# Weight folds turned by TensorE instead of through DRAM, and a new order of all stages, in a kernel of two linear-attention layers and two expert layers

## The chip, the cores and the metric

The kernel runs on one core of a Trainium2 chip. The metric is the device time of one execution in microseconds (us), the median of several runs. The engines are TensorE (PE in the profile, its weight loads PEld), VectorE (DVE), ScalarE (ACT), GpSimd (POOL) and SyncE (SP), which here only issues transfers (DMAs).

## The reference

A batch of one, 2048 rows x of width 576, passes four layers, A, B, A, B, with the same weights in both A and in both B. All arithmetic is fp32.

```python
def A(x):                                  # linear attention, 32 heads of 18
    q, k, v = heads(layernorm(x) @ wqkv)
    pq, pk = phi(q), phi(k)                # phi(t) = (t + 1 if t > 0 else exp(t)) + 1e-6
    kv = einsum("bhsd,bhse->bhde", pk, v)  # a sum over all 2048 rows
    z = pk.sum(over rows)
    o = einsum("bhqd,bhde->bhqe", pq, kv) / (einsum("bhqd,bhd->bhq", pq, z) + 1e-6)
    return x + rows(o) @ wo

def B(x):                                  # 32 heads choose one of 8 x 8 experts each
    y = layernorm(x)
    q = einsum("nd,dhc->nhc", y, w_q)      # two halves of 128 per head
    s1, s2 = q[..., :128] @ k1.T, q[..., 128:] @ k2.T
    e = 8 * argmax(s1) + argmax(s2)        # per row and head; the softmax over one choice is 1
    out = einsum("nhk,nhk,nhkd->nd", 1, gelu(y . u[e]), v[e])
    return x + out
```

## The kernel before

The 2048 rows are cut into 16 tiles of 128 rows (t = 0 to 15). Layers A and B of a pair are joined into "layer" l = 0 or 1 in the names, so that a name such as `x10_9` is buffer x1 of layer 0, tile 9. In a layer A first all tiles give their share of the state (stages f, k, v, st, and q, whose result pq waits in DRAM or in the core); when the state is complete, it is multiplied into the output weight (M), and the tiles go on one by one: ld (loads of x and pq), num (division by the denominator), oT (o is turned), O (output product and residual, x1), bT (layernorm, turned), S (scores of layer B), sel and gel (choice of expert, gelu), cT (the 64 coefficients turned), po (product with the expert values, residual x2), keep (x2 stored to DRAM). As soon as a tile of layer 0 is through, its layer-1 front (f, k, v, st) can follow.

Precision: a product of fp32 operands is done as products of halves. `split` makes them: hi is a rounded copy on ACT (L117), lo the difference on DVE (L118). A projection of a tile is 14 passes of two column parts, 28 matmuls: `ppk`, `ppv`, `ppq` (L258), `ppo` of O (L483). S is 14 matmuls (L525, its PSUM tile is called `kva` or `pps` in the profile), the state `kva` is L360, po L609.

TensorE needs the rows turned (columns on the partitions). There are two ways, and a table by tile chooses between them. `transposed`: five transposes on TensorE (L215) into PSUM, then the split. `squares`, by way of `moved`: DVE transposes the 32 x 32 squares (L229, result `r...`), one store (L231) of 320 KB takes them to DRAM (`y_d...`), four loads (L237) of 80 KB bring them back in another place (`g...`), then the split. So `rb`, `y_db`, `gb`, `thib`, `tlob` are the steps of operand b, `ro` ... `tloo` of o, `rf` ... `tlof` of f. In layer 0 the operand b goes by squares for tiles 5, 7, 9, 11 and 13.

The weights of S are made by the kernel itself: w_q (loaded in 64 pieces by `fold_load`, L631) is multiplied with the keys (`fold_mm`, L641, `fold_ps` in PSUM), in four chunks. `fold_out` (piece `fo`) copies a chunk to the core's memory (`foldf`, ACT L647 to L649), turns it by `moved` (`rfold`, `y_dfold`, `gfold`), and splits it to `shi` (ACT, L658) and `slo` (DVE, L662 and L664).

The order is written out by hand. `in_order(*ALL)` holds PE, ACT, DVE and POOL to the order of the program, and SP issues transfers in the order of the program too, one after the other. `play(text)` takes a list of pieces, "name layer.tile", and runs the next step (up to the next yield) of each, or n steps for "xn". There are four parts: a Python loop for the front tiles 2 to 9, then three texts: front tiles 10 to 15 and back tiles 0 to 4; a text that is played four times, for s = 5, 7, 9, 11 (numbers are relative to s, two tiles a turn); and the rest, with all of the second layer.

PSUM has four tiles of 128 x 1024; one holds the state while it is summed up, the others rotate.

Of the kernel before, what the change touches and what calls it, by code (L numbers as in the profile page):

```python
# [64 lines left out]
def network(ctx, tc, x_in, wqkv, wo, wq_t, k_t, u_t, v2, c_mask, c_mask4, c_ident, c_code, c_code1, c_scale, c_shift, out):  # L65
    nc = tc.nc
# [781 lines left out]
    with in_order(*ALL):

        play("""  # L850
            fT0.11 v0.10 k0.10 fT0.11x2 v0.10 fl0.13 fo0.3 ln0.13 ln0.12 fo0.3 q0.10 v0.10 q0.10 fT0.12 k0.11 k0.10
            v0.11 fT0.12 fT0.13 v0.11x2 q0.11 k0.11 fo0.3 fT0.12 st0.11 fT0.13 st0.10 fl0.15 lv0.0 fl0.14 k0.12 q0.11
            ln0.15 ld0.1 k0.12 fT0.13 v0.12x2 ln0.14 q0.12 fT0.14 q0.13 fT0.15 k0.13 fT0.14 v0.12 q0.12 k0.13 v0.13
            fT0.14 q0.13 k0.14 v0.13 fT0.15 v0.14 v0.13 st0.13 fT0.15 k0.14 st0.12 k0.15 sv0.0 ld0.0 v0.15 wl0.0 v0.14
            k0.15 v0.14 st0.14 v0.15x2 st0.15 mk0.0 zs0.0x2 num0.1 num0.0 M0.2x2 M0.3 ld0.2 num0.1 M0.3 num0.0x2 M0.1
            q0.14 oT0.0 num0.1 M0.1 num0.2 ld0.3 M0.0 M0.4 oT0.0 M0.0 oT0.1 M0.4 num0.2 oT0.1 O0.0x4 ld0.4 num0.2 O0.1
            oT0.2 num0.3 O0.1 num0.4 bT0.0 oT0.2 num0.3 bT0.0 O0.2 O0.1 S0.0 num0.3 num0.4 q0.14 O0.1 oT0.3 O0.2 ld0.6
            S0.0 bT0.1 ld0.5 num0.4 O0.2 gel0.0 sel0.0 oT0.3 sel0.0 bT0.1 q0.15 O0.2 sel0.0 gel0.0 q0.15 S0.1 O0.3
            sel0.0 S0.1 sel0.1x2 cT0.0 bT0.2 cT0.0 O0.3 num0.5 ld0.7 oT0.4 po0.0x2 gel0.1 bT0.2 S0.2 gel0.1 po0.0
            oT0.4 S0.2 sel0.1x2 O0.4 O0.3 sel0.2 po0.0 gel0.2 cT0.1 fT1.0 cT0.1 sel0.2 fT1.0 po0.1 gel0.2 v1.0 po0.1  # L860
            O0.3 sel0.2 po0.1 sel0.2 cT0.2 bT0.3 O0.4 bT0.3 po0.1 O0.4 k1.0 v1.0 cT0.2 k1.0 fT1.1 num0.5 fT1.1 S0.3
            po0.2 keep1.0 S0.3 po0.2 sel0.3x2 k1.1 num0.6 gel0.3 po0.2 v1.0 sel0.3 gel0.3 k1.1 v1.1 O0.4 bT0.4 sel0.3
            cT0.3 po0.2 v1.1x2 fT1.2 num0.6 num0.5 cT0.3 bT0.4 oT0.5 S0.4 oT0.5 O0.5 num0.6 fT1.2 st1.0 S0.4 O0.5x2
            keep1.1 st1.1 oT0.6 po0.3 oT0.6 keep1.2 O0.5
        """)
# [9 lines left out]
    with in_order(*ALL):

        play("""
            po0.11 gel0.12 bT0.13 sel0.12 po0.11x2 num0.15 sel0.12 v1.10 sel0.12 fT1.11 bT0.13 gel0.12 sel0.12 oT0.14
            k1.10 fT1.11 k1.10 v1.10 cT0.12 v1.10 num0.15 O0.14 num0.15 oT0.15 cT0.12 bT0.13 fT1.11 po0.12 S0.13
            po0.12x2 S0.13 oT0.15 O0.14 sel0.13x2 v1.11 gel0.13 O0.14 po0.12 fT1.12 gel0.13 oT0.15 O0.14 sel0.13x2  # L880
            k1.11 v1.11 O0.15 fT1.12 bT0.14 O0.15 cT0.13 st1.10 v1.11 cT0.13 bT0.14 S0.14 fT1.12 k1.11 po0.13 O0.15
            S0.14 gel0.14 po0.13 gel0.14 po0.13 keep1.12 k1.12 v1.12 sel0.14 st1.11 sel0.14 ldx1.3 po0.13 fT1.13
            sel0.14 k1.12 O0.15 v1.12 sel0.14 v1.12 cT0.14 bT0.15 cT0.14 bT0.15 po0.14 st1.12 po0.14 S0.15 fT1.13
            po0.14 fT1.13 S0.15 v1.13 ldx1.1 sel0.15 po0.14 fT1.14 v1.13 sel0.15x2 gel0.15 k1.13 gel0.15 sel0.15
            fT1.14 cT0.15 bT0.-1 v1.13 cT0.15 v1.14 po0.15 bT0.-1 k1.13 q1.13 v1.14 po0.15 q1.13 po0.15x2 ldq1.13
            v1.14 k1.14 wl1.0 st1.13 fT1.15x2 k1.15 v1.15 k1.14 rl1.0 st1.14 k1.15 v1.15x2 st1.15 rl1.1 lq1.0 mk1.0
            lq1.0 zs1.0 M1.1x2 zs1.0 rl1.3 M1.4x2 M1.3 num1.13 lq1.1 M1.0 ldx1.0 num1.0 num1.13 num1.0x2 M1.3 keep1.11
            lq1.1 num1.1 oT1.0 M1.0 oT1.0 num1.1 M1.2x2 rl1.2 rl1.4 lq1.2 O1.0 num1.1 oT1.1 num1.13 oT1.13 q1.14 lq1.2
            O1.0 oT1.1 O1.0x2 lq1.3 num1.2 q1.14 lq1.3 oT1.13 bc1.0,-9 O1.1 bc1.0,-9 num1.2 num1.3 O1.1 num1.2 S1.0
            oT1.2 S1.0 num1.3 oT1.2 lq1.4 ldx1.5 gel1.0 num1.3 O1.1x2 O1.2 bc1.1,-9 sel1.0 gel1.0 ldx1.2 sel1.0 lq1.4  # L890
            O1.13 bc1.1,-9 num1.4 rl1.6 sel1.0 num1.4 S1.1 ldx1.13 lq1.6 O1.2x2 num1.4 rl1.5 O1.13 rl1.7 S1.1 sel1.0
            O1.2 sel1.1 O1.13 ldq1.14 gel1.1 bc1.2,0 lq1.5 rl1.8 oT1.4 bc1.2,0 lq1.6 oT1.3 sel1.1x2 O1.13 gel1.1 S1.2
            oT1.3 po1.0 lq1.5 sel1.1 po1.0 S1.2 O1.3 sel1.2 rl1.9 num1.6 O1.3 bc1.13,1 num1.5 lq1.7 gel1.2 bc1.13,1
            sel1.2 num1.5 gel1.2 num1.5 oT1.4 S1.13 lq1.7 O1.3x2 rl1.11 sel1.2 po1.1 sel1.2 oT1.5 q1.15 ldx1.4 po1.1
            bc1.3,2 num1.6 S1.13 gel1.13 oT1.5 num1.6 ldx1.6 bc1.3,2 rl1.10 ldx1.7 sel1.13 q1.15 O1.4 po1.2 num1.14
            O1.5 po1.2 oT1.6 sel1.13 O1.4x2 ldq1.15 sel1.13 num1.7 S1.3 num1.14 num1.7 gel1.13 num1.14 S1.3 sel1.13
            O1.4 O1.5 sel1.3 lq1.8 num1.7 ldx1.14 sel1.3 oT1.6 gel1.3 bc1.4,13x2 O1.6 lq1.8 O1.5 oT1.7 po1.13 O1.5
            sel1.3 rl1.12 num1.8 po1.13 O1.6 S1.4 ldx1.8 gel1.3 num1.8 sel1.3 oT1.7 S1.4 gel1.4 sel1.4x2 bc1.5,3
            oT1.14 lq1.9 O1.6 sel1.4 bc1.5,3 S1.5 O1.6 ldx1.11 num1.8 ldx1.15 po1.3 oT1.8 gel1.4 oT1.14 num1.15 S1.5
# [9 lines left out]
            O1.11 sel1.15 oT1.12 S1.10 gel1.10 bc1.11,15 sel1.10 bc1.11,15 O1.12 po1.9 gel1.10 O1.12 S1.11 sel1.10  # L909
            O1.12 sel1.10 po1.15 sel1.10 S1.11 sel1.11x2 base1.10 O1.12 bc1.12,10x2 gel1.11 S1.12 sel1.11 gel1.11  # L910
            S1.12 sel1.11 gel1.12x2 po1.10 base1.11 bc1.-1,11 sel1.12 bc1.-1,11 base1.12 sel1.12x2 po1.10 po1.11
            sel1.12 po1.11 po1.15 bc1.-1,12x2 po1.12x2
        """)


# [42 lines left out]
```

## Time and profile before

| what | value |
|---|---|
| median of 3 runs | 741.06 us (739.82 to 742.75) |
| the profiled execution | 738.86 us, span 737.1 us |
| mean granted TensorE clock | 0.993 |
| instructions | 14704, of them 5444 matmuls |
| moved by DMA | 109.79 MB, mean 149 GB/s |

The span is what the profiler saw between the first and the last instruction; the time of the execution has 1.8 us around it. Stretches of the span: 0 to 180 holds the front of layer 0 with its folds, 180 to 300 the first back tiles, 300 to 440 the loop's four turns, 440 to 520 the end of layer 0's back, 520 to 737 layer 1's back. A row of a timeline reads: start, length, engine, line, operation, output <- inputs, shapes, how many in a row, and in brackets how long the engine had been idle before it and on what. In tables of lines the columns are busy time, mean ns of one, idle time just before and what ended it.

### The profile page before, as it was taken

The numbers are of one execution on the slowest core, as the hardware profiler recorded it, in microseconds if no ns is written. First come the engines' busy times: TensorE is split into PE (matmuls) and PEld (weight loads), VectorE is DVE, ScalarE is ACT, GpSimd is POOL, SyncE is SP. The second block draws the span as 40 slices with busy tenths as digits, with TensorE's granted clock in tenths as the row PEclk, the third lists the DMA queues.
The fourth block names the chain that finished last, engine by engine and source line by source line (L and its number), as shares of the span: only waits on it lengthen the run. The fifth ranks groups of instructions, "written<-read, shape, count | busy, mean of one in ns | idle before, by whom it ended". The sixth has DMA issues, their size and how long they took to land.

```text
span 737.1 us, 14704 instructions
## 1 busy us (share of the span) xinstructions
PE 707.6 (96%) x5444; PEld 651.7 (88%) x5444; DVE 483.5 (66%) x1035; ACT 322.4 (44%) x658; POOL 200.9 (27%) x543
## 2 busy tenths in 40 slices
PE   9999999989999999998999898999999999999995
PEld 6999899879999998887988898989999999999984
DVE  5643444425427877787777788662356789998996
ACT  4423332323324456445444554454444543545443
POOL 2211001010004433334243332320123433533431
PEclk9999999999999999999999999999999999999999
DMA  9848887875412222565756656532634323121101
GB/s 261 258 155 258 269 273 255 263 224 149 129 33 76 86 100 91 170 201 178 220 173 220 182 192 204 171 92 69 181 87 120 105 85 117 49 81 49 33 33 64
DMA packets 85591, 109.79 MB, mean 149 GB/s; under 512 B 9296, under 2 KB 49744, under 8 KB 85520
## 3 DMA queue, kind: packets, MB, share of 16 engines
q1 hardware_dynamic: 85520, 108.86, 47.8%
q8 instruction: 43, 0.70, 0.4%
q14 instruction: 28, 0.23, 0.1%
HBM read 70.19 MB, written 38.63 MB: 148 GB/s over the span
## 4 chain that ended last, share of the span: by engine, by line
PE 65%; DMA 11%; DVE 10%; ACT 5%; issue 3%; SPq 3%; POOL 2%; ACTq 0%; DVEq 0%; POOLq 0%
PE ppq L258 13%; PE ppo L483 11%; PE ppk L258 9%; PE pps L525 9%; PE ppv L258 8%; PE kva L525 3%; SPq L237 3%; DMA gf<-y_df 2%; DMA y_df<-rf 2%; PE ptb L215 2%; PE kva L360 2%; PE po L609 2%; PE pto L215 2%; DMA y_db<-rb 1%; DMA y_dfold<-rfold 1%
## 5 line engine op out<-in xcount | busy, mean ns | idle before, releaser
L483 PE MATMUL ppo<-ohi,thio 126*128 126x252 f32 (+1 forms) x320 | 50.5, 300 | 2.0 <-ACT thio L117 1.4
L188 ACT ACTIVATE junk<-x,mb 128x576 bf16<-128x576 f32 x32 | 24.8, 775 | 56.3 <-POOL mb L187 56.2
L258 PE MATMUL ppk<-whi,thif 128*128 128x252 f32 (+1 forms) x300 | 45.6, 299 | 2.8 <-ACT v L320 1.7
L483 PEld LDWEIGHTS ppo<-ohi,thio 126*128 126x128 f32 (+1 forms) x320 | 44.8, 189 | 3.9 <-ACT thio L117 1.8
L258 PEld LDWEIGHTS ppk<-whi,thif 128*128 128x128 f32 x300 | 40.9, 188 | 6.5 <-issue 2.9
L179 POOL TENSOR_SCALAR rsf<-mvf 128x1 f32<-128x1 f32 x16 | 3.4, 211 | 158.5 <-DVE mvf L176 158.4
L258 PE MATMUL ppv<-whi,thif 128*128 128x252 f32 (+1 forms) x300 | 44.6, 295 | 1.3 <-ACT thif L117 1.2
L258 PE MATMUL ppv<-whi,tlof 128*128 128x252 f32 (+1 forms) x300 | 43.9, 293 | 0.0
L258 PE MATMUL ppk<-whi,tlof 128*128 128x252 f32 (+1 forms) x300 | 43.9, 293 | 0.0
L258 PEld LDWEIGHTS ppv<-whi,thif 128*128 128x128 f32 x300 | 41.2, 188 | 2.7 <-ACT thif L117 2.0
L453 POOL TENSOR_TENSOR o<-pq,zb 128x576 f32<-128x576 f32 x19 | 27.4, 1444 | 55.0 <-ACT zb L399 52.4
L205 ACT ACTIVATE yb<-x,rsb 128x640 f32<-128x640 f32 x32 | 29.4, 920 | 26.9 <-POOL rsb L195 26.9
L258 PEld LDWEIGHTS ppk<-whi,tlof 128*128 128x128 f32 x300 | 41.2, 188 | 0.0
L258 PEld LDWEIGHTS ppv<-whi,tlof 128*128 128x128 f32 x300 | 41.2, 188 | 0.0
L118 DVE TENSOR_TENSOR tlof<-gf,thif 128x640 fp32r<-128x640 f32 x23 | 18.9, 822 | 33.0 <-ACT thif L117 33.0
L258 PE MATMUL ppq<-whi 128*128 128x252 f32 (+1 forms) x260 | 39.6, 299 | 0.0
L483 PE MATMUL ppo<-olo,thio 126*128 126x252 f32 (+1 forms) x256 | 39.6, 293 | 0.0
L483 PE MATMUL ppo<-ohi,tloo 126*128 126x252 f32 (+1 forms) x256 | 39.5, 293 | 0.0
L277 DVE TENSOR_SCALAR eq<-eq 128x576 f32<-128x576 f32 x19 | 8.8, 462 | 46.4 <-ACT eq L276 46.4
L258 PEld LDWEIGHTS ppq<-whi 128*128 128x128 f32 x260 | 36.0, 188 | 0.7 <-DVE eq L287 0.3
L205 ACT ACTIVATE yf<-xf,rsf 128x640 f32<-128x640 f32 x15 | 13.8, 922 | 51.9 <-POOL rsf L181 51.9
L483 PEld LDWEIGHTS ppo<-olo,thio 126*128 126x128 f32 x256 | 36.2, 188 | 0.0
(204 smaller groups left out, 1834.7 us busy)
## 6 DMA issues: line engine op xcount, KB each, us to landing
fold<-in_wq_t SPq DMA_DIRECT2D x64, 288.0 KB
...
```

Source lines behind the costliest of these rows:

```text
L118: eng.tensor_tensor(lo, src, hi.bitcast(F32), op=ALU.subtract)
L188: nc.scalar.activation(junk, xt, AF.Square, bias=m[:, 0:1], accum_out=m[:, 1:2])
L205: nc.scalar.activation(y, x2, AF.Identity, scale=rs[:, 0:1], bias=rs[:, 1:2])
L215: nc.tensor.transpose(pt[:, b * P:(b + 1) * P], x, ident)
L237: nc.sync.dma_start(g[32 * j:32 * j + 32], d.rearrange("(q i) (j x) -> j i q x", q=4, j=4)[j])
L258: nc.tensor.matmul(o[:, at:at + c1 - c0], tt[a == "lo"][:, b, :], wb[:, cols + c0:cols + c1], start=(i == 0), stop=(i == len(todo) - 1))
L277: nc.vector.tensor_scalar(e, e, 1.0, EPS, op0=ALU.min, op1=ALU.add)
L360: nc.tensor.matmul(a[64 * h:64 * h + 64, c * 72:c * 72 + n], vt[:, 2 * c + h], fk[:, f0:f0 + n], start=(t == 0 and c == 0), stop=(t == NT ...
L453: nc.gpsimd.tensor_tensor(o[:, :D], pq, zb, op=ALU.mult)
L483: nc.tensor.matmul(p[:, at:at + c1 - c0], hl[a][:r, b], w[:r, c0:c1], start=(i == 0), stop=(i == len(todo) - 1))
L525: nc.tensor.matmul(p[:, :512], hl[a == "lo"][:, b, :], shi[:, b] if w == "hi" else slo[:, blocks(REM)[b][1]], start=(i == 0), stop=(i == l ...
L609: nc.tensor.matmul(p[:, at:at + c1 - c0], c[i], vmix[:, c0:c1], start=(i == 0 and not based), stop=(i == 1))
```

## The change

First, `fold_out` doesn't call `moved` any more. Five `nc.tensor.transpose` turn a chunk into a PSUM tile `fold_pt`, from which the same copies and differences to `shi` and `slo` are taken. That removes 4 DVE transposes, 4 stores and 16 loads, and adds 20 TensorE transposes. In the Python loop `fold_out` has a step less. Second, all three texts are written anew: the same pieces with the same counts but for `fo`, in another order; the table of what is turned by which way stays.

```diff
@@ -647,13 +647,15 @@
         nc.scalar.activation(f[:, :320], p[:, :320], AF.Copy)
         nc.scalar.activation(f[:, 320:384], p[:, 256:320], AF.Copy)
         nc.scalar.activation(f[:, 384:], p[:, 512:768], AF.Copy)
-        g = yield from moved(f, f"fold{ch}")
-        yield
+        yield
+        pt = psum(f"fold_pt{ch}")
+        for b in range(NB):
+            nc.tensor.transpose(pt[:, b * P:(b + 1) * P], f[:, b * P:(b + 1) * P], ident)
 
         def dst(w, b):
             return w[:, b, :448].rearrange("p (e c a j) -> p c j a e", e=E - 1, c=4, a=4)[:, ch]
 
-        src = [g.rearrange("p j (b a e) -> p b j a e", b=NB, a=4)[:, b, :, :, 1:] for b in range(NB)]
+        src = [pt[:, b * P:(b + 1) * P].rearrange("p (j a e) -> p j a e", j=4, a=4)[:, :, :, 1:] for b in range(NB)]
         for b in range(NB):
             nc.scalar.activation(dst(shi, b), src[b], AF.Copy)
         for b, (r, bl) in enumerate(blocks(REM)):
...
@@ -841,75 +843,73 @@
             if done is not None:
                 run(0, (fo, done, 1))
             run(0, (v, t), (q, t), (fT, t + 1), *pair(t))
-            if done is not None:
-                run(0, (fo, done))
             for m in groups:
                 fold_mm(m)
     with in_order(*ALL):
...
-            v1.-3 po0.-2 bT0.0 gel0.-1 bT0.0 sel0.-1 po0.-2x2 num0.2 gel0.-1 k1.-3 sel0.-1 fT1.-2 oT0.1 sel0.-1 num0.2
...
+            bT0.0 num0.2 po0.-2 sel0.-1x2 gel0.-1 bT0.0 po0.-2x2 v1.-3 gel0.-1 v1.-3 k1.-3 sel0.-1 fT1.-2 oT0.1
...
```

TensorE's own order changes in few places: the fold's transposes come in; v comes before k for odd front tiles of layer 1; in the loop the transpose `ptc` of cT of an odd tile (5, 7, 9, 11) comes before the 28 matmuls `ppo` of O and not behind them; in the end of layer 0's back `ppo` of tile 14 comes before `ptc` of tile 12. On the other engines and in the queue much more is moved. Three places follow.

The queue (SP) in the loop's turn for tiles 9 and 10, around the store of b of tile 9 (`y_db0_9`); `hl_d6` is the store of f's halves of tile 6, `x_d7` the store of x2 of tile 7. Before:

```order
L231 DMA y_do0_10_4667<-ro0_10_4665 128x640
L237 DMA go0_10_4720<-y_do0_10_4667 32x4x160 x4
L436 DMA x0_12_4906<-in_x 128x576
L333 DMA hl_d6_94<-thif1_6_4711 128x640
L334 DMA hl_d6_94<-tlof1_6_4712 128x640
L617 DMA x_d7_143<-x20_7_4801 128x576
L231 DMA y_db0_9_4807<-rb0_9_4805 128x640
L237 DMA gb0_9_4813<-y_db0_9_4807 32x4x160 x4
```

And in the changed kernel:

```order
L231 DMA y_do0_10_4665<-ro0_10_4663 128x640
L441 DMA pq0_12_4891<-pq_d0_12_116 128x576
L333 DMA hl_d6_94<-thif1_6_4649 128x640
L436 DMA x0_12_4889<-in_x 128x576
L237 DMA go0_10_4752<-y_do0_10_4665 32x4x160
L334 DMA hl_d6_94<-tlof1_6_4650 128x640
L237 DMA go0_10_4752<-y_do0_10_4665 32x4x160 x3
L231 DMA y_db0_9_4762<-rb0_9_4760 128x640
L617 DMA x_d7_143<-x20_7_4766 128x576
L237 DMA gb0_9_4788<-y_db0_9_4762 32x4x160 x4
```

The store of b moved ahead of that of x2; one store of f's halves, the load of x, and a load of pq moved ahead of the four loads `go`.

VectorE in the same turn, the way to `cg0_7`, the coefficients that `ptc0_7` turns. Before:

```order
L581 TENSOR_REDUCE pi0_7_4632<-pr0_7_4630 128x16
L118 TENSOR_TENSOR tloo0_9_4551<-go0_9_4545,thio0_9_4550 128x640
L229 STREAM_TRANSPOSE rf1_6_4640<-yf0_6_4616 128x5x4x32
L456 TENSOR_REDUCE den0_10_4644<-o0_10_4592 128x32
L584 TENSOR_TENSOR ct0_7_4650<-pi0_7_4632,shift_71 128x64
L587 TENSOR_SCALAR c20_7_4652<-ct0_7_4650 128x64
L590 TENSOR_TENSOR cg0_7_4654<-g0_7_4594,c20_7_4652 128x128
```

And in the changed kernel:

```order
L456 TENSOR_REDUCE den0_10_4615<-o0_10_4487 128x32
L229 STREAM_TRANSPOSE rf1_6_4618<-yf0_6_4538 128x5x4x32
L574 TENSOR_TENSOR oh0_7_4629<-cd0_7_4601,code_w_70 128x256
L577 TENSOR_TENSOR pr0_7_4631<-oh0_7_4629,m20_7_4599 128x512
L581 TENSOR_REDUCE pi0_7_4633<-pr0_7_4631 128x16
L584 TENSOR_TENSOR ct0_7_4635<-pi0_7_4633,shift_71 128x64
L587 TENSOR_SCALAR c20_7_4637<-ct0_7_4635 128x64
L590 TENSOR_TENSOR cg0_7_4639<-g0_7_4547,c20_7_4637 128x128
L118 TENSOR_TENSOR tloo0_9_4613<-go0_9_4607,thio0_9_4612 128x640
```

The difference `tloo0_9`, which O waits for, moved behind `cg0_7`; the sums `den` and the transpose `rf` moved to the front of oh, pr and pi. Not shown: the transpose `rb0_8` moved from ahead of `mt0_7` to behind `m0_7`, still ahead of `cg0_7`.

ScalarE at the last fold, around 157 to 165 us of the trace before; `v5_0` are the copies of v, of which the third is L320, and the product for the next k takes its PSUM tile. Before:

```order
L117 ACTIVATE thif0_11_2030<-gf0_11_2025 128x640
L318 ACTIVATE v5_0_86<-ppv0_10_1967 128x4x63 x2
L647 ACTIVATE foldf3_2038<-fold_ps3_1769 128x320
L648 ACTIVATE foldf3_2038<-fold_ps3_1769 128x64
L649 ACTIVATE foldf3_2038<-fold_ps3_1769 128x256
L205 ACTIVATE yf0_13_2055<-xf_13_2036,rsf0_13_2051 128x640
L205 ACTIVATE yf0_12_2066<-xf_12_1813,rsf0_12_2062 128x640
L320 ACTIVATE v5_0_86<-ppv0_10_1967 128x2x36
L276 ACTIVATE eq0_10_2103<-ppq0_10_2073 128x576
```

And in the changed kernel:

```order
L318 ACTIVATE v5_0_86<-ppv0_10_1954 128x4x63 x2
L205 ACTIVATE yf0_13_2058<-xf_13_2016,rsf0_13_2054 128x640
L320 ACTIVATE v5_0_86<-ppv0_10_1954 128x2x36
L205 ACTIVATE yf0_12_2070<-xf_12_1804,rsf0_12_2066 128x640
L117 ACTIVATE thif0_11_2077<-gf0_11_2072 128x640
L276 ACTIVATE ek0_10_2083<-ppk0_10_1987 128x576
L647 ACTIVATE foldf3_2087<-fold_ps3_1760 128x320
L648 ACTIVATE foldf3_2087<-fold_ps3_1760 128x64
L649 ACTIVATE foldf3_2087<-fold_ps3_1760 128x256
L660 ACTIVATE shi_80<-fold_pt3_2091 128x4x4x7 x5
L276 ACTIVATE eq0_10_2117<-ppq0_10_2020 128x576
```

The copies of v and the layernorms `yf` moved ahead of `thif0_11`, which waits for its loads, and of the fold's copies.

More of the change, by code (lines that the diff above doesn't have):

```diff
@@ L861, in network @@
[L861 to L864, printed above, removed]
+            v0.10 fT0.11 k0.10 fl0.13 v0.10 q0.10 ln0.13 v0.10 ln0.12 fT0.11x2 fl0.15 k0.10 fo0.3x2 lv0.0 q0.10 wl0.0
@@ L865, in network @@
+            po0.2 S0.3 po0.2 sel0.3 keep1.0 sel0.3 k1.1 gel0.3 sel0.3 gel0.3 po0.2 k1.1 v1.1 O0.4 bT0.4 sel0.3 cT0.3
+            po0.2 v1.1x2 fT1.2 num0.5 cT0.3 bT0.4 oT0.5 S0.4 fT1.2 oT0.5 S0.4 keep1.1 num0.6 O0.5 keep1.2 po0.3 num0.6
+            O0.5 oT0.6 O0.5x2 st1.0 oT0.6 st1.1
         """)
@@ L908, in network @@
-            O1.10 sel1.9 sel1.15 gel1.15x2 bc1.10,9 num1.12 O1.11 sel1.15 bc1.10,9 O1.11 oT1.12 S1.10 sel1.15 po1.9
[L909 to L912, printed above, removed]
+            gel0.12 bT0.13 po0.11 sel0.12 v1.10 po0.11x2 gel0.12 num0.15 sel0.12 k1.10 bT0.13 v1.10 sel0.12 fT1.11
@@ new lines, in network @@
+            q1.14 lq1.3 oT1.13 bc1.0,-9 num1.3 O1.1 bc1.0,-9 num1.2 O1.1 num1.2 S1.0 oT1.2 S1.0 num1.3 lq1.4 gel1.0
+            num1.3 oT1.2 O1.1x2 O1.2 bc1.1,-9 sel1.0 gel1.0 ldx1.2 sel1.0 lq1.4 O1.13 rl1.6 bc1.1,-9 sel1.0 num1.4x2
+            S1.1 O1.2 num1.4 O1.2 ldx1.13 O1.13 S1.1 lq1.6 O1.2 sel1.0 sel1.1 bc1.2,0 rl1.5 ldx1.5 rl1.7 gel1.1
+            ldq1.14 lq1.5 lq1.6 bc1.2,0 oT1.4 gel1.1 oT1.3 sel1.1 O1.13 rl1.8 sel1.1 S1.2 po1.0 oT1.3 lq1.5 sel1.1
+            S1.2 O1.3 po1.0 sel1.2 rl1.9 O1.13 oT1.4 num1.6 bc1.13,1 num1.5 sel1.2 num1.5 lq1.7 bc1.13,1 gel1.2x2
@@ new lines, in network @@
+            bc1.8,14 num1.10 lq1.11 bc1.8,14 po1.14 sel1.7 O1.9 lq1.11 O1.9 po1.14 gel1.7x2 sel1.7 S1.8 sel1.7 O1.15
+            bc1.9,7 S1.8 ldx1.12 gel1.8 sel1.8 num1.11 O1.15 oT1.10 gel1.8 sel1.8 bc1.9,7 lq1.12 O1.15 S1.9 sel1.8
+            oT1.10 num1.11 sel1.8 lq1.12 O1.15 num1.12 po1.7 S1.9 num1.11 bc1.15,8 gel1.9 po1.7 sel1.9 O1.10 num1.12
+            gel1.9 oT1.11 bc1.15,8 O1.10 po1.8x2 O1.10 sel1.9 oT1.11 S1.15x2 O1.10 sel1.9 O1.11 sel1.9 gel1.15x2
+            sel1.15 bc1.10,9 num1.12 O1.11 sel1.15 bc1.10,9 O1.11 oT1.12 S1.10 sel1.15 po1.9 O1.11 sel1.15 oT1.12
@@ L913, in network @@
+            S1.10 gel1.10 bc1.11,15 sel1.10 O1.12 po1.9 gel1.10 bc1.11,15 O1.12 S1.11 sel1.10 O1.12 sel1.10 po1.15
+            sel1.10 S1.11 sel1.11x2 base1.10 O1.12 bc1.12,10x2 gel1.11 S1.12 base1.11 gel1.11 sel1.11 S1.12 sel1.11
+            gel1.12 po1.15 sel1.12 gel1.12 po1.10 bc1.-1,11x2 base1.12 sel1.12 po1.11 sel1.12 po1.10 sel1.12 po1.11
+            bc1.-1,12x2 po1.12x2
         """)
```

78 lines of the change are left out of this document (34 added, 44 removed).

## The prediction

> **What bounds the kernel now.** I read the busy times first, then the busy time by stretch, then the waits of TensorE, then the chain that ended last, and last the timelines of the queue (SP) and the engines around one turn of the loop. The first row is the page's, the others are from the table by stretches, in whose columns the stretch's length comes first.
>
> ```profile
> PE 707.6 (96%) x5444; PEld 651.7 (88%) x5444; DVE 483.5 (66%) x1035; ACT 322.4 (44%) x658; POOL 200.9 (27%) x543
> ...
> core 0: us, PE busy (x) PEld busy (x) DVE busy (x) ACT busy (x) POOL busy (x), PEclk, DMA share, GB/s
> ...
> 120.00:180.00 60.00, 56.96 (x499) 51.70 (x498) 25.82 (x52) 17.87 (x44) 4.02 (x12) 1.00 0.73 225
> ...
> 300.00:440.00 140.00, 130.97 (x955) 119.54 (x953) 108.66 (x231) 70.24 (x148) 50.68 (x133) 0.98 0.63 196
> 440.00:520.00 80.00, 74.63 (x599) 70.72 (x599) 45.54 (x101) 39.84 (x85) 18.48 (x55) 1.00 0.41 129
> 520.00:700.00 180.00, 180.00 (x1262) 169.32 (x1261) 143.72 (x312) 83.51 (x156) 67.75 (x175) 1.00 0.31 91
> 700.00:737.10 37.10, 28.86 (x162) 24.02 (x161) 29.34 (x84) 14.58 (x30) 10.40 (x33) 0.96 0.13 48
> ...
> 340.00:360.00 20.00, 17.80 (x113) 16.40 (x112) 15.58 (x32) 9.67 (x22) 7.65 (x20) 0.91 0.65 206
> ```
>
> TensorE is the bound, and it idles 737.1 − 707.6 = 29.5 us in all: 9.0 in 300 to 440, which is the loop of four turns, 5.4 in 440 to 520, 3.0 in 120 to 180, 8.2 in the tail. From 520 to 700 it never idles, so a new order there can win nothing. A change of order is worth at most these gaps, and 340 to 360 shows a second item: the granted clock is 0.91 there. The next rows are TensorE's waits (in all, times, longest) and pieces of the chain (start, length, what).
>
> ```profile
> PE kva L525 <- ACT thib L117: 5.4, 4, 2.1
> PE ptc L512 <- DVE cg L590: 4.1, 4, 1.8
> PE ppk L258 <- ACT v L320: 1.7, 1, 1.7
> PE fold_ps L641 <- DMA fold<-in_wq_t: 0.7, 2, 0.4
> PE ppq L258 <- ACT foldf L649: 0.7, 1, 0.7
> ...
> 347.79 5.08 PE kva L525 x14
> 409.84 4.91 DMA y_db<-rb
> 419.25 5.07 PE kva L525 x14
> 436.86 3.27 PE kva L525 x14
> ```
>
> The largest wait is at the score matmuls S (L525) of the loop's odd tiles, 5.4 us. Behind two of these waits the 14 matmuls take 5.08 and 5.07 instead of 3.27, another 3.6 us. Together 9.0 us. The chain goes there through the store y_db of the turned operand b, 4.91 us long.
>
> **Part 1: the way to S of the odd tiles.** The queue's rows of one turn, then VectorE's transpose that feeds the store, then the wait it ends in:
>
> ```profile
> 366.73 0.38 SPq L231 DMA_DIRECT2D y_do<-ro  x1
> 369.77 1.73 SPq L237 DMA_DIRECT2D go<-y_do  x4
> 371.60 0.38 SPq L436 DMA_DIRECT2D x<-in_x  x1
> 372.07 0.38 SPq L333 DMA_DIRECT2D hl_d<-thif  x1
> 372.54 0.38 SPq L334 DMA_DIRECT2D hl_d<-tlof  x1
> 372.98 0.49 SPq L617 DMA_DIRECT2D x_d<-x  x1
> 373.56 0.99 SPq L231 DMA_DIRECT2D y_db<-rb  x1
> 379.12 1.75 SPq L237 DMA_DIRECT2D gb<-y_db  x4
> ...
> 371.39 0.84 DVE L229 STREAM_TRANSPOSE rb<-yb 128x640 f32<-128x640 f32 x1
> ...
> 383.36 1.43 PE L525 MATMUL kva<-shi,thib 128*128 128x512 f32 x5 [1.69 <-ACT thib L117]
> ...
> 419.25 2.06 PE L525 MATMUL kva<-shi,thib 128*128 128x512 f32 x5 [1.45 <-ACT thib L117]
> ```
>
> rb is ready at 371.39 + 0.84 = 372.23, and its store leaves at 373.56, 1.33 us late, because the queue is issuing four other transfers one by one. It is then followed by its loads 5.56 us after its issue; the store y_do, with nothing freshly ahead of it, by its own after 3.04. The new order puts one hl_d store, x and a pq load into the time in which the queue waits for y_do, and x_d behind y_db. So the store gains at least the 1.33 us, and at most 1.33 + (5.56 − 3.04) = 3.85. Bytes that are still in front (the go loads and one hl_d store) speak against the full gain; the transpose rb, which also moves ahead of the residual x20, speaks for more than the least. The waits are 2.1 (the longest), 1.69, 1.45 and the remaining 0.2: the low bound leaves 0.8, 0.4 and 0.1 of them, 1.3 of 5.4, the high bound nothing. I take the nearer to the high one: 4.4 of the wait and the 3.6 of slow matmuls, **−8.0** (bounds −4.0, if the slow matmuls stay too, and −9.0).
>
> The clock's part can be weighed. In this trace the 14 matmuls are slow after two waits at S, and the third wait, 1.69 us, is followed by five in 1.43. [...]
>
> **Part 2: the other waits of the loop.** 9.0 of idle less the 5.4 leaves 3.6 in many short waits for operands v, O and k. The go loads now stand behind three more transfers of about 0.3 MB each, the f transposes stand earlier. Bounds: all of it goes, −3.6; or those 0.9 MB, at the 196 GB/s of the loop's row 4.6 us, delay go by what y_do's 3.04 us of landing don't cover, 1.6 a turn, and O with it, +6 in four turns. The first is nearer, since O's waits are short now and the transposes rf and rb come earlier: **−1.0**.
>
> **Part 3: cT (ptc, L512) of odd tiles now ahead of O (L483).** TensorE then waits for cg before it may start O, where before 28 matmuls of O lay between.
>
> ```profile
> 361.35 1.58 PE L483 MATMUL ppo<-ohi,thio 126*128 126x252 f32 x10
> ...
> 354.87 1.40 DVE L553 TENSOR_TENSOR mt<-s 128x256 f32<-128x256 f32 x1
> 360.22 0.83 DVE L118 TENSOR_TENSOR tloo<-go,thio 128x640 fp32r<-128x640 f32 x1
> 360.97 0.84 DVE L229 STREAM_TRANSPOSE rf<-yf 128x640 f32<-128x640 f32 x1
> 362.97 0.29 DVE L590 TENSOR_TENSOR cg<-g,c 128x128 f32<-128x128 f32 x1
> 372.15 0.38 DVE L553 TENSOR_TENSOR mt<-s 128x256 f32<-128x256 f32 x1
> ...
> DVE rf L229 <- ACT yf L205: 11.3, 7, 2.5
> DVE rb L229 <- ACT yb L205: 2.0, 3, 1.3
> ```
>
> TensorE would stand at ptc at 361.35, when it starts O now; cg ends at 363.26. With VectorE as it is that is 1.9 us. tloo moves behind cg and takes its 0.75 of that chain, and mt, 1.40 here, is 0.38 in the next tile. So 0.2 to 1.15, I take 0.7 for each of four odd tiles: **+2.8**. The bounds are nothing at all, and 1.9 with the longest waits for yf and yb, 2.5 and 1.3, whose transposes now stand in cg's chain: 5.1 less tloo's 0.75, 4.3 each, 17 in all. Behind the waiting ptc stand O, then S; behind O the residual, yb and the next store.
>
> **Part 4: after the loop.** O of tile 14 now precedes ptc of tile 12. ptc's four waits make 4.1, of which the longest is 1.8; these lie mostly here. One of them is covered by O's 28 matmuls: **−1.6** (bounds 0 and −4.1).
>
> **Part 5: around 157 to 165.** The last copy of v stood on ACT behind the fold's copies and behind a thif that waits for a load. In the new order it comes ahead of both. The waits 1.7 (ppk for v) and 0.7 (ppq for foldf) go, and of the fold loads' 0.7 a half, since the queue has no more y_dfold to wait for: **−2.7** (bounds −0.5 and −3.1).
>
> **Part 6: the fold's transposes.** Four stores, 16 loads and four transposes of VectorE (0.85 each) go; they lie in a stretch where VectorE is busy 25.82 of 60, so they cost nothing now but the queue's time, counted above. Twenty TensorE transposes come, on the bound engine.
>
> ```profile
> 544.77 1.09 PE pto L215 x10
> L215 PE MATMUL pto<-ident,o 128*128 128x128 f32 x110 | 15.4, 273 | 0.8 <-DVE o L461 0.4 <-ACT thib L117 0.4
> L658 ACT ACTIVATE shi<-gfold 128x112 fp32r<-128x112 f32 x20 | 5.2, 448 | 12.6 <-DMA gfold<-y_dfold 12.6
> ```
>
> Ten in a row take 1.09 in the chain, 0.109 each, so 20 cost **+2.2**. The mean of one is 273 ns, but busy times overlap in a stream; the upper bound is 20 x 0.273 = 5.5. The copies shi stay (5 x 0.448 for each chunk) and read what TensorE wrote without the 12.6 us of waiting for loads. The PSUM tile they hold is asked for again only after a product of 28 matmuls (3.9 us and more), and 2.2 us of copies with as much of slo beside it are over by then.
> [...]
>
> Nothing is won in 520 to 700. In the tail VectorE is busy 29.34 of 37.1 and its work stays: 0.
>
> **Sum.** −8.0 − 1.0 + 2.8 − 1.6 − 2.7 + 2.2 = −8.3. Against the profiled execution's 738.86 (span 737.1 and 1.8 around it) that is 730.6. That execution was 2.2 below the median of 741.06, so the forecast is 741.06 − 8.3 = **732.8**.
>
> **Rivals.**
> 1. *It all clears.* The loop's idle time and slow matmuls (9.0 + 3.6), all 3.1 around 157 to 165, half of the 5.4 after the loop, cT at nothing, less 2.2 of transposes: −16.2, 724.9. For it: the order was made with the transfers in mind, and every gap named has a cause in it. Against: ptc's place is new and worse by the rows.
> 2. *The store lands no sooner.* The bytes ahead travel with it; only 1.33 of issue is won, S gives 4.0 and the clock stays, cT costs 1.15 each: −4.0 − 1.0 + 4.6 − 1.6 − 2.7 + 2.2 = −2.5, 738.6, no change. For it: three transfers come ahead of the go loads.
> 3. *The slow matmuls stay though the waits go*: −8.3 + 3.6 = −4.7, 736.4.
> 4. *Slower: TensorE stands at ptc.* Place: cT of tiles 5, 7, 9, 11. Without part 3 the sum is −11.1, so it decides from 11.1/4 = 2.8 us a tile. At 4.3 (above) it gives −11.1 + 17.2 = +6.1, 747.2. For it: yf was waited for up to 2.5 us with less in VectorE's way. Against: the mean of those seven waits is 1.6, and most of rf's waits fall where VectorE has nothing else to do.
>
> **How the numbers follow.** A difference within 0.5% (737.4 to 744.8) is about what a measurement of this kernel cannot tell from no change. Forecast 0.47 (its own range 728 to 737); all clears 0.12; slow matmuls stay 0.10; no change 0.18; slower 0.13. Of the third rival and of the forecast a little lies above 737.4. So faster 0.67, same 0.20, slower 0.13. The range leaves out the better half of rival 1 and rival 4 with its price: 724 to 742.
>
> **What would show it.** Right: no wait of TensorE over 1 us for thib at odd S; the 14 matmuls of S at 3.27 throughout; the clock 1.00 in 340 to 360 and 420 to 440; gaps ahead of ptc of 0.2 to 1.2; y_db followed by its loads in under 4.5 us; no gap at 157 to 165; five fold transposes in 0.46 to 0.55. Wrong: ptc's waits over 8 us in total, y_db's way unchanged at 5 to 5.6, or gaps of TensorE in the last layer, where it had none.

## The result and the profile after

The changed kernel takes 721.4 us (median of 4 runs, 720.9 to 722.1), the kernel before 741.8 beside it; the ratio is 0.973 (95% interval 0.971 to 0.975), 20 us less. The forecast was 732.8 with a range of 724 to 742, so the change gave more than twice what was forecast. The profiled execution is 720.9 against 738.9, 18.0 less.

First the busy times, then the table by stretches, then TensorE's waits, all of the changed kernel. Its events lie up to 18 us earlier than before, so the stretches hold slightly later work.

```profile
PE 698.8 (97%) x5464; PEld 649.9 (90%) x5464; DVE 474.0 (66%) x1031; ACT 320.9 (45%) x658; POOL 202.7 (28%) x543
...
120.00:180.00 60.00, 59.88 (x552) 56.89 (x545) 26.19 (x55) 19.91 (x47) 6.46 (x18) 1.00 0.66 209
...
300.00:440.00 140.00, 134.95 (x1034) 126.27 (x1034) 115.22 (x252) 78.51 (x164) 55.41 (x143) 1.00 0.67 211
440.00:520.00 80.00, 77.99 (x626) 72.78 (x625) 41.43 (x89) 40.54 (x84) 16.41 (x45) 1.00 0.46 136
520.00:700.00 180.00, 179.28 (x1223) 168.64 (x1222) 148.84 (x339) 80.91 (x154) 69.05 (x193) 1.00 0.24 74
...
PE ppo L483 <- ACT thio L117: 3.9, 4, 1.4
PE ptb L215 <- DVE cg L590: 3.2, 2, 2.7
...
PE ptc L512 <- DVE cg L590: 0.6, 2, 0.4
```

In 120 to 180 the idle time fell from 3.0 to 0.1. The wait for `thib` at S in the loop, 5.4 us before, is gone from the list; a wait of O for `thio` has come, 3.9 us in four. For the loop the stretches must hold the same work, so the next two rows go from the end of O of tile 5 to the end of v of tile 10, first in the kernel before, then in the changed one:

```profile
297.19:445.25 148.06, 139.03 (x1058) 127.45 (x1059) 114.72 (x242) 74.54 (x157) 53.95 (x142) 0.98 0.62 192
```

```profile
291.79:429.38 137.59, 133.41 (x1059) 125.08 (x1058) 110.66 (x244) 75.38 (x157) 54.61 (x142) 1.00 0.68 216
```

TensorE idles 4.2 us there where it idled 9.0, and is busy for 5.6 us less with the same matmuls. So more than half of the loop's gain is matmuls that no longer run long; the granted clock is 1.00, not 0.98.

Where the 18.0 us arose is read by lining up the ends of the same matmuls in both traces: 4.9 at the end of layer 0's state, 5.4 when O of tile 5 ends (before the loop), 15.9 when v of tile 10 ends, 18.6 when v of tile 15 ends, 18.0 at the last matmul. So 4.9 in the front, 0.5 in 217 to 297, 10.5 in the loop, 2.7 behind it; layer 1 gives nothing and takes 0.6. The forecast had 0.5, 0, 6.2 and 1.6.

Two statements ahead of the forecast have to be corrected. Operand b goes through DRAM for all tiles 5 to 13 of layer 0, the even ones too; the largest waits lay at odd tiles all the same. And the piece `keep` stores f's halves (`hl_d`); x2 is stored (`x_d`) in `po`. The edits below are read with that.

### The profile page after: what moved, and what is told of

It reads as the page before. It is cut to its first block, busy times and chain, and to the rows that moved or that the text cites. A ratio compares the mean times of both kernels' runs of the same rounds, so it can differ in the third digit from the quotient of the medians.

```text
span 719.1 us, 14715 instructions
## 1 busy us (share of the span) xinstructions
PE 698.8 (97%) x5464; PEld 649.9 (90%) x5464; DVE 474.0 (66%) x1031; ACT 320.9 (45%) x658; POOL 202.7 (28%) x543
## 5 line engine op out<-in xcount | busy, mean ns | idle before, releaser
L277 DVE TENSOR_SCALAR ek<-ek 128x576 f32<-128x576 f32 x16 | 7.4, 460 | 46.2 <-ACT ek L276 46.2
L258 PE MATMUL ppk<-wlo,thif 128*128 128x252 f32 x240 | 36.1, 293 | 0.0
L258 PE MATMUL ppv<-wlo,thif 128*128 128x252 f32 x240 | 36.1, 293 | 0.0
```

Of the source, the lines that this page charges most:

```text
L258: nc.tensor.matmul(o[:, at:at + c1 - c0], tt[a == "lo"][:, b, :], wb[:, cols + c0:cols + c1], start=(i == 0), stop=(i == len(todo) - 1))
L277: nc.vector.tensor_scalar(e, e, 1.0, EPS, op0=ALU.min, op1=ALU.add)
```

## The experiments

Times are medians, ratios are to runs of the kernel before on the same chip (medians 742.1 to 743.3). The first four split the change into its places.

**Only the fold.** `fold_out` as in the change, all texts old:

```diff
-            v0.11 fT0.12 fT0.13 v0.11x2 q0.11 k0.11 fo0.3 fT0.12 st0.11
+            v0.11 fT0.12 fT0.13 v0.11x2 q0.11 k0.11 fT0.12 st0.11
```

> Only the fold is changed (TensorE turns the chunks), all three texts keep their old order. Theory: in the kernel before, four of the eight groups of fold matmuls took 2.81, 2.63, 3.65 and 3.72 us where all take 2.18 in the changed kernel, since their loads stood in the queue behind the round trip of a fold chunk; without the round trip these 4.1 us go whatever the order, 20 transposes cost 2.2 (0.56 for five), the wait 0.7 for the fold's copies goes, the wait 1.7 for v's copy stays: -2.6 us against before. Rival: the groups are late because of the order of the other transfers; then only the 2.2 of the transposes are added and the time is 1.5 to 2.2 us above before.

Measured: 745.2, ratio 1.003 (1.001 to 1.006), 2.4 us slower by the ratio: about the rival's time, but not for the rival's reason. The fold matmuls' rows (busy time of L641; columns as in the table by stretches) of the kernel before, then of this run:

```profile
110.00:136.00 26.00, 5.96 (x64) 2.74 (x64) 1.00 0.80 263
136.00:200.00 64.00, 3.33 (x32) 1.41 (x32) 1.00 0.62 185
```

```profile
110.00:136.00 26.00, 4.37 (x64) 2.18 (x64) 1.00 0.76 242
136.00:200.00 64.00, 2.18 (x32) 1.09 (x32) 0.97 0.53 159
```

These 96 fold matmuls are busy for 6.55 us, not 9.29; with 0.6 in an earlier group and the 0.7 of idle time between them, 4.1 us are gone. The loads are in time in the old order too, so the round trip had held them up. The list of waits before showed only the 0.7 of it; the rest stood as busy time of this line. That gain, and more, is then lost: the end of the state comes 0.6 us later than in the trace before, mostly by the 2.2 of transposes and by this one place. TensorE and ScalarE there:

```profile
156.09 0.71 PE L653 MATMUL fold_pt<-ident,foldf 128*128 128x128 f32 x5
160.64 2.59 PE L258 MATMUL ppq<-whi,thif 128*128 128x252 f32 x10 [3.85 <-ACT v L320]
...
157.32 0.92 ACT L205 ACTIVATE yf<-xf,rsf 128x640 f32<-128x640 f32 x1 [2.03 <-POOL rsf L181]
158.59 0.92 ACT L205 ACTIVATE yf<-xf,rsf 128x640 f32<-128x640 f32 x1 [0.35 <-POOL rsf L181]
159.41 1.11 ACT L660 ACTIVATE shi<-fold_pt 128x112 fp32r<-128x112 f32 x5
160.33 0.26 ACT L320 ACTIVATE v<-ppv 128x72 f32<-128x72 f32 x1
```

The transposes take one more PSUM tile. The next product then needs the tile of v, whose last copy stands on ScalarE behind two layernorms that wait for GpSimd, and behind the fold's own copies: TensorE waits 3.85 us, and its next matmuls run more slowly for a while (ten take 2.59, elsewhere 1.46 to 1.6). In the changed kernel v's copy comes ahead and the transposes stand behind the product for q, and there is no wait. Each five transposes cost 0.55 us in the rows of matmul ends, 2.2 in all, as forecast. The rest of the 2.4 lies behind the front; the run with the new order of the front comes back to it.

**That loss alone.** The same with one piece moved, the split of f of tile 11 behind the fold's copies:

```diff
-            fT0.11 v0.10 k0.10 fT0.11x2 v0.10 fl0.13 fo0.3 ln0.13 ln0.12 fo0.3 q0.10
+            fT0.11 v0.10 k0.10 fT0.11 v0.10 fl0.13 fo0.3 ln0.13 ln0.12 fo0.3 fT0.11 q0.10
```

> The fold by TensorE in the old order (the first run), with one piece moved: the split of f of tile 11, whose hi copy waits for loads on ScalarE, comes behind the last fold's copies, not ahead of them. In the first run TensorE waited 3.85 us for a PSUM tile behind the last fold's transposes and the 28 matmuls then took 5.5 instead of 3.9 us. Theory (the fold's copies stood behind that hi copy, and the transposes hold a PSUM tile until they are done): both go, 5 us less than the first run, 2 to 3 us less than before. Rival: the wait only moves on to the next product (ppk of tile 11, for thif): no more than 2 us less than the first run.

```profile
158.71 1.59 PE L258 MATMUL ppq<-whi,thif 128*128 128x252 f32 x10 [1.88 <-ACT v L320]
...
156.87 1.14 ACT L660 ACTIVATE shi<-fold_pt 128x112 fp32r<-128x112 f32 x5 [1.15 <-PE fold_pt L653]
157.80 0.74 ACT L117 ACTIVATE thif<-gf 128x640 fp32r<-128x640 f32 x1
158.43 0.22 ACT L320 ACTIVATE v<-ppv 128x72 f32<-128x72 f32 x1
```

Measured: 741.2, ratio 0.998 (0.996 to 1.001), not clear of no change. The end of the state comes 3.5 us earlier than in the first run: half of the wait is gone and the slow matmuls with it. The other half stays: ScalarE is through with the layernorms, but v's last copy now stands behind the fold's own copies `shi`, which wait for the transposes, and behind the `thif` that was moved. So the theory was right in part.

**The fold and the new order of the front alone.** The first text up to the end of the state is new, everything behind it old:

```diff
-            fT0.11 v0.10 k0.10 fT0.11x2 v0.10 fl0.13 fo0.3 ln0.13 ln0.12 fo0.3 q0.10 v0.10 q0.10 fT0.12 k0.11 k0.10
...
+            v0.10 fT0.11 k0.10 fl0.13 v0.10 q0.10 ln0.13 v0.10 ln0.12 fT0.11x2 fl0.15 k0.10 fo0.3x2 lv0.0 q0.10 wl0.0
...
```

> The fold by TensorE and the new order of the front of layer 0 (first text up to the end of the state), all later order old. Theory that the gains lie side by side: as much as the two traces differ at the end of the state, 4.9 us less than before. Rival: part of it is given back later, since the loop and the stage before it wait for transfers and not for TensorE; then less than 3 us is left.

Measured: 740.4, ratio 0.995 (0.993 to 0.997), 3.6 us less, between the theory's 4.9 and the rival's 3. Its trace has 5.1 at the end of the state and still 5.1 when O of tile 5 ends. Its loop, the old one, then took 153.1 us against 148.1 in the profiled execution before (from O of tile 5 to v of tile 10). Four traces have the old loop: 148.1, 150.9, 151.9 and 153.1.

Two things lie in this. The profiled execution on which the forecast was built was a short one: its 738.9 lies under the medians of 742 to 743. And the three longer loops are those of the three runs with the fold on TensorE. In them O of tiles 9, 11 and 13 waits 0.6 to 1.6 us each; with the fold through DRAM, in the kernel before and in the run with y_db ahead of x_d below, it waits 0.6 at most. All three runs also end with 1.5 to 1.8 us less gain than their traces have at the end of the state (3.6 for 5.1 here, −2.4 for −0.6 in the first, 1.4 for 2.9 in the second). Each difference is no wider than its interval, so this is a hint, not a proof: the fold on TensorE seems to cost something in the loop. Why is open; the four tiny stores below try one cause.

**All behind the front.** The front and the fold are old; the first text from the end of the state on, the loop's and the last are new. The seam:

```diff
-            mk0.0 zs0.0x2 num0.1 num0.0 M0.2x2 M0.3
...
+            ld0.2 ld0.3 mk0.0 zs0.0x2 num0.0 M0.2x2 num0.1 M0.3x2
...
```

> The fold by way of DRAM and the old order up to the end of layer 0's state, the new order from there on. Theory that the gains lie side by side: 13.1 us less than before (18.0 less the front's 4.9). Rival: the new order behind the state needs the front's; then less than 10 us.

Measured: 726.7, ratio 0.977 (0.974 to 0.980), 17.2 us less by the ratio, more than the theory's 13.1, which was taken from the short profiled execution. With the 3.6 of the front that is 20.8 against 20 for the whole: within the intervals the parts add up, nothing needs both.

**The loop alone.** Only the text that is played four times is new:

```diff
-            v1.-3 po0.-2 bT0.0 gel0.-1 bT0.0 sel0.-1 po0.-2x2 num0.2 gel0.-1 k1.-3 sel0.-1 fT1.-2 oT0.1 sel0.-1 num0.2
...
+            bT0.0 num0.2 po0.-2 sel0.-1x2 gel0.-1 bT0.0 po0.-2x2 v1.-3 gel0.-1 v1.-3 k1.-3 sel0.-1 fT1.-2 oT0.1
...
```

> Only the text of the loop (played four times) is new, the fold and the two other texts are the old ones. Theory: the loop's gain is its own, S of odd tiles no longer waits (5.2 us), its 14 matmuls no longer take 5.1 (3.6 us), and the short waits shrink: 9 to 10.5 us less than before. Rival: it depends on how far the tiles have come when the loop begins, or is given back in the stretch behind the loop; then 4 to 7 us less.

Measured: 730.4, ratio 0.982 (0.978 to 0.986), 13.2 us less; the theory's 9 to 10.5 lies at the edge of the interval. Its loop takes 135.8 us. Part is given back behind it, where the text is still old:

```profile
437.85 0.30 PE L512 MATMUL ptc<-ident,cg 128*128 128x128 f32 x1 [1.16 <-DVE cg L590]
439.22 2.78 PE L483 MATMUL ppo<-ohi,thio 126*128 126x252 f32 x10 [1.07 <-ACT v L320]
```

TensorE waits at ptc of tile 12, then O of tile 14 waits for v's last copy, and ten matmuls of O take 2.78. The new last text, which has O ahead of ptc, and the little ahead of the loop make the difference to the run before this one: 3.7 us between the two medians.

The next runs ask what in the loop's text does it.

**The store y_db ahead of x_d, in the old loop.**

```diff
-            v1.-3 po0.-2 bT0.0 gel0.-1
+            v1.-3 bT0.0 po0.-2 gel0.-1
```

> The kernel before, with one thing moved in the loop: the transpose rb of odd tiles and its store y_db come ahead of the residual x2 and its store x_d (tile s-2), nothing else. Theory (the store's place in the queue makes S of odd tiles wait): the store leaves 0.5 to 1.3 us earlier with one transfer of 0.29 MB less ahead, some 2 us in all, so the waits of 1.5 to 2.1 us at three odd S and the slow matmuls behind them nearly go: 6 to 8 us less than before. Rival (the bytes of the two hl_d stores ahead, or the engines' own chains, set it): less than 3 us.

Measured: 740.1, ratio 0.997 (0.996 to 0.999): 2 us less, the rival. The queue, with rb ready at 372.29 + 0.85 = 373.14:

```profile
372.29 0.85 DVE L229 STREAM_TRANSPOSE rb<-yb 128x640 f32<-128x640 f32 x1 [0.47 <-ACT yb L205]
...
373.52 0.38 SPq L334 DMA_DIRECT2D hl_d<-tlof  x1
373.95 0.49 SPq L231 DMA_DIRECT2D y_db<-rb  x1
374.54 1.04 SPq L617 DMA_DIRECT2D x_d<-x  x1
379.55 1.74 SPq L237 DMA_DIRECT2D gb<-y_db  x4
```

The store leaves half a us sooner after rb, and its loads follow 6.4 us after rb where they followed 6.9. From the store's issue to its loads it is 5.6 us as before, though x_d now stands behind it and not ahead. It stays behind the x load and both hl_d stores. The waits at S fell all the same, to 1.15, 0.51 and 0.28, since rb too stands earlier (S comes 10.1 us after it, not 9.4), but waits of 0.6 at ptc of the even tiles came.

**The store ahead of the hl_d stores too.** `in_order` gets SP as well in the loop. Without it the transfers aren't put into the program in the order of the text, but by what is ready:

```diff
-    with in_order(*ALL):
+    with in_order(*ALL, ET.SP):
-            v1.-3 po0.-2 bT0.0 gel0.-1
+            v1.-3 bT0.0 po0.-2 keep1.-3 gel0.-1
...
-            oT0.3 S0.1 st1.-2 O0.2 fT1.-1 keep1.-1 S0.1 po0.0 O0.2
+            oT0.3 S0.1 st1.-2 O0.2 fT1.-1 S0.1 po0.0 O0.2
```

> The kernel before, with the store y_db of odd tiles moved ahead of x_d and of both hl_d stores in the loop, and the queue held to the order of the text there (x and pq loads of a tile then come a little later). Theory: no S of an odd tile waits, all of its 14 matmuls take 3.5 us: 8 to 10 us less than before, and no more than 3 us less than the run with x_d alone moved. Rival: with S free another operand (o or f) is late next in the old order and takes back more than half.

```profile
377.93 0.34 SPq L231 DMA_DIRECT2D y_db<-rb  x1
...
380.12 2.41 SPq L237 DMA_DIRECT2D gb<-y_db  x4
...
PE ppv L258 <- ACT thif L117: 12.3, 4, 3.4
```

Measured: 750.6, ratio 1.011 (1.006 to 1.015), slower. The store is now followed by its loads after 2.2 us, and no odd S waits. But in the order of the text x and pq stand ahead of the f loads, and TensorE waits 12.3 us for f. What the rival said came: S free, another operand late. How much of the loss is the holding itself isn't known: no run has the old loop held to the text and nothing else moved.

**The hl_d stores back behind go, in the new loop.** The control is the changed kernel with the queue held to the text:

```diff
-    with in_order(*ALL):
+    with in_order(*ALL, ET.SP):
```

> The changed kernel with the queue held to the order of the text in the loop (the changed kernel leaves it to readiness there, so that x_d and y_db stand among the loads go). It is the control of the next run. Theory: the go loads come together but the f loads stand behind x and pq, one gain and one loss: between 1 us less and 5 us more than the changed kernel's 721.4; no wait of TensorE at S of odd tiles.

Measured: 723.1, ratio 0.972 (0.969 to 0.975), as expected. On top of it:

```diff
-            bT0.0 num0.2 po0.-2 sel0.-1x2
+            po0.-2 bT0.0 num0.2 sel0.-1x2
-            S0.1 keep1.-1 st1.-2 O0.2 cT0.0 O0.2 po0.0 oT0.3 S0.1
+            S0.1 st1.-2 O0.2 cT0.0 O0.2 po0.0 oT0.3 keep1.-1 S0.1
```

> As the control (queue held to the text in the loop), with the transfers of odd turns put where the kernel before has them: both hl_d stores behind the four go loads, and x_d ahead of y_db. Theory: the 0.64 MB of the hl_d stores ahead of y_db set when it lands, wherever x_d is; y_db is followed by its loads 2.5 to 4 us later than in the control, TensorE waits 1 to 2 us at three or four odd S, and some of the 14 matmuls behind it take 5 us: 4 to 10 us more than the control. Rival: VectorE's new order (rb ahead of x2, splits of f early) has made the room, so S doesn't wait: within 2 us of the control.

```profile
PE ppv L258 <- ACT thif L117: 3.8, 3, 1.8
PE ppo L483 <- ACT thio L117: 3.6, 4, 1.2
```

Measured: 729.3, ratio 0.980 (0.978 to 0.983), 6.1 us more than the control. The time is in the range of the theory, but the place is the rival's: S of odd tiles waits 0.14 once, and f and O wait, twice with slow matmuls behind. The loads of b follow rb 0.9 to 2.1 us later than in the control, not 2.5 to 4. In the control `thib` is ready 1.35 us ahead of S at tiles 7, 9 and 11; here it is 0.6 ahead, 0.1 late and 0.6 ahead. That margin takes up what the store loses; the queue's delay falls on those operands that have no margin.

**ptc behind O again**, TensorE's order alone, in the changed kernel:

```diff
-            num0.3 cT0.0 ld0.4 oT0.3 O0.2 k1.-2 O0.2
+            num0.3 ld0.4 oT0.3 O0.2 cT0.0 k1.-2 O0.2
```

> The changed kernel, with the transpose ptc of odd tiles put back behind the 28 matmuls of O in the loop, TensorE's order alone. Theory: the place doesn't matter, since cg is ready when TensorE comes there and nothing waits for the coefficients that soon: within 1.5 us of the changed kernel (721.4). Rival 1 (the prediction's step): ptc ahead of O costs 0.7 each, so this is 2.8 faster. Rival 2: coefficients, x2 and the next f come earlier by ptc's place, and the loop's gain rests on it: 4 us slower or more.

```profile
PE ppo L483 <- ACT thio L117: 5.5, 5, 1.7
```

Measured: 723.2, ratio 0.975 (0.971 to 0.979), 1.8 more than the changed kernel's median and 1.7 in the two spans (720.8 and 719.1). The two ratios' intervals overlap, so the size is not certain, but the 2.8 faster of rival 1 is out. In the traces O waits 5.5 us in the loop here and 3.9 in the changed kernel: TensorE would wait for O's operand anyhow, and ptc fills a part of that. The place of ptc is no cost, and more likely a small gain.

**Four tiny stores.** In `fold_out` of the changed kernel:

```diff
+        nc.sync.dma_start(dr.tile([P, 16], F32, name=f"shift_d{ch}"), ident[:, :16])
```

> The changed kernel with four tiny stores (8 KB, one a fold chunk) added in the front; the order of all else is the same. In the run with the fold by way of DRAM, O of tiles 9, 11 and 13 waited 0.1, 0.0 and 0.3 us, in the changed kernel 0.83, 0.89 and 0.83. The kernel with the fold on TensorE has 20 transfers less, which shifts which of the eight completion counters each later transfer uses by four; four stores shift it back. Theory: the counters' turn makes the last go load leave later; with it shifted back O's waits in the loop fall below 0.3 each: 1.5 to 2.5 us less than the changed kernel. Rival: it doesn't matter: within 0.7 us of it.

Measured: 722.1, ratio 0.970 (0.968 to 0.973): the rival. The trace of the kernel before has 518 transfers of SP, whose landings are counted on eight counters in turn, that of the changed kernel 498. In this run's trace O of tiles 9, 11 and 13 waits 0.76, 1.43 and 1.30, so the counters' turn is not the cause. Why O of tiles 9 to 13 waits 0.83 to 0.89 in the changed kernel, and hardly where only the text behind the front is new, stays open.

**The go loads together.** In the changed kernel:

```diff
-            po0.-1 keep1.-2 v1.-2
+            po0.-1 oT0.2 keep1.-2 v1.-2
...
-            gel0.0 oT0.2 v1.-2 num0.3
+            gel0.0 v1.-2 num0.3
```

> The changed kernel with the loads go of odd tiles earlier in the loop's text, so that in the queue the last three go loads stand together ahead of the store y_db, which before stood between the second and the third. Theory: the last go load, which O of tiles 7, 9, 11 and 13 waits for, leaves 0.4 to 1 us earlier, and S of the even tiles, whose operand was ready 0.7 us ahead of its use, bears the later y_db: O's three waits of 0.83 to 0.89 us shrink by half or more, 1 to 2.5 us less than the changed kernel (721.4). Rival: what is taken from O is given to S of even tiles or to f, so the time stays within 0.7 us.

```profile
388.13 1.43 PE L525 MATMUL kva<-shi,thib 128*128 128x512 f32 x5 [0.49 <-ACT thib L117]
...
421.07 1.43 PE L525 MATMUL kva<-shi,thib 128*128 128x512 f32 x5 [1.06 <-ACT thib L117]
```

Measured: 721.4, ratio 0.970 (0.967 to 0.974), the changed kernel's time. O of tiles 9 to 13 no longer waits (0.1 at most), S of even tiles waits instead, up to 1.06. So the rival held: this place in the queue is only exchanged.

## Why the prediction was wrong, point by point

The direction and the places were right; the sum was −8.3 where −18.0 (profiled executions) and −20 (medians) were measured. By the runs: front −3.6, loop −13.2, the rest −4.0. Between the two profiled executions 9.7 us are missing from the sum: 3.8 in the fold loads (part 5), 2.8 at ptc (part 3), 1.9 at S (part 1) and 1.1 behind the loop (part 4). Only part 3 had the mechanism wrong; the others were sized too small.

- *Part 1, S of odd tiles, −8.0.* The size was near: 5.2 of waits and the 3.6 of slow matmuls are gone, and 1.1 more at S of tiles 5, 6, 9 and 10, 9.9 in all. Of the two moves that the forecast counted together, x_d behind the store and hl_d, x and pq into the wait for y_do, the first alone gave 2 us. What else stands ahead weighs more, which I had only against the full gain: with x and both hl_d stores in front the loads follow 6.4 us after rb, with none 2.2. In the changed kernel one hl_d store leaves while the queue waits for y_do, the other behind the first of the loads go, and the store of b leaves at once:

```profile
354.76 0.34 SPq L231 DMA_DIRECT2D y_do<-ro  x1
355.19 0.55 SPq L441 DMA_DIRECT2D pq<-pq_d  x1
356.72 0.32 SPq L333 DMA_DIRECT2D hl_d<-thif  x1
357.13 0.38 SPq L436 DMA_DIRECT2D x<-in_x  x1
357.62 0.37 SPq L237 DMA_DIRECT2D go<-y_do  x1
358.08 0.42 SPq L334 DMA_DIRECT2D hl_d<-tlof  x1
358.55 1.54 SPq L237 DMA_DIRECT2D go<-y_do  x3
361.04 0.34 SPq L231 DMA_DIRECT2D y_db<-rb  x1
361.70 0.34 SPq L617 DMA_DIRECT2D x_d<-x  x1
364.42 1.75 SPq L237 DMA_DIRECT2D gb<-y_db  x4
```

  The loads follow 3.4 us after the store, 5.6 before, and pq, hl_d and x cost y_do nothing (its first load leaves after 2.9 us). But the queue is not the whole cause. With both hl_d stores and x_d put back ahead of the store, S of odd tiles still hardly waited: there, and in the changed kernel, VectorE is through with rb 5.5 to 6.3 us after O of the same tile, in the kernel before 7 to 8 (tiles 7, 9 and 11). How the gain divides between the queue and VectorE's order is not measured.
- *Part 2, the loop's other waits, −1.0.* The old short waits went and new ones came (O of tile 6 waits 1.40, of 9, 11 and 13 0.83 to 0.89), about as weighed: beside S the whole loop gained 0.6 us, ptc included.
- *Part 3, ptc ahead of O, +2.8.* This step failed, in sign too. VectorE, TensorE and the wait that followed, in the changed kernel:

```profile
349.98 0.29 DVE L590 TENSOR_TENSOR cg<-g,c 128x128 f32<-128x128 f32 x1
...
350.41 0.33 PE L512 MATMUL ptc<-ident,cg 128*128 128x128 f32 x1
351.57 1.59 PE L483 MATMUL ppo<-ohi,thio 126*128 126x252 f32 x10 [0.83 <-ACT thio L117]
```

  cg is there 0.14 us ahead of TensorE, at the other odd tiles of the loop 0.06 to 0.12; TensorE waited there once, 0.23 us. What I had wrong is the length of VectorE's chain in the new order. I took the chain of one turn before and let it shrink by tloo's 0.75 and by the 1.40 that mt took, since mt takes 0.38 in the next tile. But 1.40 against 0.38 is odd tile against even tile: mt takes 1.39 to 1.40 at tiles 7, 9 and 11 of the kernel before, as here at tile 9, where S was not slow.

```profile
389.89 1.39 DVE L553 TENSOR_TENSOR mt<-s 128x256 f32<-128x256 f32 x1
```

```profile
343.18 0.42 DVE L553 TENSOR_TENSOR mt<-s 128x256 f32<-128x256 f32 x1
```

  The first of these rows is tile 9 of the kernel before, the second tile 7 of the changed one. From the end of S to the end of cg it takes 10.4 to 12.4 us at tiles 5, 7, 9 and 11 before, and 8.4 to 8.8 in the changed kernel. With the old chain cg would have come 1.9 to 3.0 us behind the start of O, so the fear had a ground; the new order of VectorE shortened the chain by more than I allowed, and the 0.1 us to spare is luck. Why mt is short at odd tiles now is open. The run with ptc put back has it the other way: 1.8 us slower, not clear of noise.
- *Part 4, behind the loop, −1.6.* Mis-sized: 2.7 by the traces, 4.0 by the runs with what lies ahead of the loop. The wait at ptc of tile 12 (1.62) was covered as forecast; that at ptc of tile 14 (1.80) fell to 0.41 and two waits on v and f (1.4) went, which the forecast did not count, and new waits of 0.5 to 0.9 took back 2.1. In three other runs O of tile 14 runs long behind the waits there (5.45 to 5.52 for 3.92); in the profiled execution before it did not.
- *Part 5, around 157 to 165, −2.7.* Both waits went as forecast. What failed is the fold loads' share: 0.3 was taken from the list of waits, 4.1 is what the groups lost (2.81, 2.63, 3.65 and 3.72 us where each takes 2.18). The first run shows it: without the round trip all eight take 2.18 in the old order too. The sizes of equal groups side by side would have shown it; the list of waits does not.
- *Part 6, transposes, +2.2.* Measured 4 x 0.55 = 2.2, where 20 times the row's mean of 273 ns would have been 5.5. The claim that the PSUM tile is not asked for again too soon holds in the new order alone: with the old one it cost 3.85 us and slow matmuls.
- *The base.* The profiled execution was a short one, and I added its 2.2 us to the median as a shift. The four runs of the changed kernel lie within 1.2 us, so the longer executions of the kernel before seem to lose time that the change takes away. Which waits they lose is not shown, since only one execution was traced.
- *Rivals.* "It all clears", 724.9 at 0.12, was the nearest and still 3.5 high. The second, that the store lands no sooner, is out: its loads follow after 3.4 us, not 5.6. The slow matmuls went with the waits, so the third is out; the fourth's wait did not come.
- *The signs.* Those named for S, the clock (1.00 in 340 to 360 and in 420 to 440), the store, 157 to 165 and the transposes came. The gaps of 0.2 to 1.2 ahead of ptc did not, but for the 0.23. Of those named for being wrong a trace of one came: TensorE has a new wait of 0.49 us in the last layer.
